# Attention and a gated feed-forward layer on one core: part of the weight conversion moved from VectorE to GpSimd, in pairs and in a new order

## The chip, the cores and the metric

The kernel runs on one core of one Trainium2 chip. The metric is the device time of one execution in microseconds, as the median of several runs. Engines are called by their names in the profile: PE (matrix multiply), DVE (VectorE), ACT (ScalarE), POOL (GpSimd), SP (the queue that issues all of this kernel's DMAs).

## The reference

```python
# q, k, v: (8, 8, 576, 64); p: (8, 8, 32, 64); w_in: (512, 2048); w_out: (2048, 512)
def sm_attn(qq, kk, vv):
    s = scale * np.matmul(qq, kk.transpose(0, 1, 3, 2))
    a = np.exp(s - np.max(s, axis=-1, keepdims=True))
    a = a / (np.sum(a, axis=-1, keepdims=True) + 1e-09)
    return np.matmul(a, vv)
p_packed = sm_attn(p, k, v)
out = sm_attn(q, p_packed, p_packed)

x = out.transpose(0, 2, 1, 3).reshape(4608, 512)
h = x @ w_in
g = h * np.tanh(softplus(h))          # Mish
return g @ w_out
```

The two weights arrive as float64; everything else is float32.

## The kernel before, in words

**Work.** There are 8 batches, and the hidden width of 2048 is cut into 16 groups of 128. The main loop makes one step `t` per batch and group: `up` multiplies the attention weights of the batch with a packed form of `w_in` (two halves `up(0)`, `up(1)`, six L627 matmuls each), ACT applies Mish (L630, L632) from PSUM, and `down` multiplies the result of an earlier group with `w_out` (four column blocks `down(0)` to `down(3)`; in batch 0 as one fp32 product, which is two L666 instructions). `LAG = 2` says that the downs of step t belong to the group of step t - 2. `packed_w(b, c)` multiplies the second attention's values into chunk c of `w_in` (four groups, 16 L577 matmuls), ACT and DVE split the product into a high and a low part (`wp_hi`, `wp_lo`). Chunks 1 to 3 of batch 0 are packed at t = 3, 7 and 11, ahead of the step that needs them. It needs two PSUM tiles of the pool `ps_a`, which also holds the scores of the next batch's attention; DVE frees those by reading them (L416, and L242 for the value product).

**Weights.** The float64 weights come as 32 pieces: `Weight(c, m)`, 16 of `w_in` (four for a chunk), and `WeightOut(i)`, 16 of `w_out` (one for a group). Each piece is 128 x 1024 words of 32 bits, with low and high words side by side. A piece goes through three steps. `fetch`: a DMA into a staging tile `w_st` (pool `stg`, `STB = 10` buffers). `words`: ACT reads the high words as floats scaled by 2^-112 into the destination (L547) and the low words, scaled by 2^-29, into a tile `wround` (L548). `join`: DVE clamps the scaled value (L552), shifts it by 3 bits (L555), ORs the sign bit from the high word in staging (L556), and adds the rounding (L559), all on 128 x 512.

**Order.** Batch 0's attention and the first four joined pieces stand before the loop (the opening). In the loop, `join_next` joins two pieces at each step t = 0 to 13, and `upto("fetch", k + 1 + STB)` fetches the piece that takes over the freed staging buffer. The pieces run wi, wi, wi, wi (chunk 0) and then wi and wo in turns, so that the last piece of chunk c is joined in the step whose `packed_w` reads it. The attention of batch 1 is a generator, moved on by `advance(gen)` three times a step from t = 2; `flush` runs the DVE work that was put off until the next point. The order on PE is the order of the program everywhere; on SP up to t = 16; on DVE and ACT from just before the loop up to t = 16. In the opening, a scheduler orders DVE and ACT.

**Loads.** Before step 0, SP also gets the first five loads for batch 1 (`load_next`: p, then k, k, q, q, v); later ones are issued as tiles come free. SP issues strictly in order, so a load stands behind every fetch written ahead of it, and a fetch behind the join that frees its buffer.

Of the kernel before, what the change touches and what calls it, by code (L numbers as in the profile page):

```python
# [10 lines left out]
I32 = mybir.dt.int32  # L11
U32 = mybir.dt.uint32
AF = mybir.ActivationFunctionType
ALU = mybir.AluOpType
# [3 lines left out]
GB = 3  # L18
KVB = 8
KQB = 5  # L20
STB = 10
OB = 2
ATT0 = 2
LOAD0 = 0
# [10 lines left out]
def body(  # L35
# [75 lines left out]
    def load_heads(src, b, g, tag):  # L111
        ts = []
        for h0 in (4 * g, 4 * g + 2):
            t = early.tile([R, 2, NI, 2 * D], F32, name=tag, tag="kvq", bufs=KVB)
            nc.sync.dma_start(
                out=t, in_=src[b, h0:h0 + 2].rearrange("h (p i x) d -> p h i (x d)", i=NI, x=2)
            )
            ts.append(t)
        return ts
# [411 lines left out]
    class Weight:  # L531
# [6 lines left out]
        def fetch(self):  # L538
            self.st = stg.tile([P, 2 * FC], I32, name="w_st")
            nc.sync.dma_start(out=self.st, in_=w_in_v[:, self.m, self.c * 2 * FC:(self.c + 1) * 2 * FC])  # L540
            self.dst = wi[self.c][self.m // 2][:, self.m % 2]

        def words(self):
            x = self.st.rearrange("p (n t) -> p n t", t=2)
            low, self.high = x[:, :, 0], x[:, :, 1]
            self.r = stg.tile([P, FC], I32, name="wround", bufs=3)
            nc.scalar.activation(out=self.dst, in_=self.high.bitcast(F32), func=AF.Copy, scale=F64_SCALE)  # L547
            nc.scalar.activation(out=self.r, in_=low.bitcast(U32), func=AF.Copy, scale=2.0 ** -29)  # L548

        def join(self):  # L550
            dst, bits = self.dst, self.dst.bitcast(I32)
            nc.vector.tensor_scalar(  # L552
                out=dst, in0=dst, scalar1=F64_HIGH, scalar2=-F64_HIGH, op0=ALU.min, op1=ALU.max
            )
            nc.vector.tensor_scalar(out=bits, in0=bits, scalar1=3, scalar2=None, op0=ALU.logical_shift_left)  # L555
            nc.vector.scalar_tensor_tensor(  # L556
                out=bits, in0=self.high, scalar=-0x80000000, in1=bits, op0=ALU.bitwise_and, op1=ALU.bitwise_or
            )
            nc.vector.tensor_tensor(out=bits, in0=bits, in1=self.r, op=ALU.add)  # L559

    class WeightOut(Weight):
        def __init__(self, i):
# [131 lines left out]
    def together(*gens):  # L694
        gens = list(gens)
        while gens:
            gens = [x for x in gens if next(x, "end") != "end"]
# [24 lines left out]
    n_groups = B * NF  # L722

    pieces = [Weight(0, m) for m in range(4)]
    for f in range(NF):
        if f < 12:
            pieces.append(Weight(1 + f // 4, f % 4))
        pieces.append(WeightOut(f))
    pieces_done = {"fetch": 0, "words": 0, "join": 0}

    def upto(step, n):
        while pieces_done[step] < min(n, len(pieces)):
            k = pieces_done[step]
            getattr(pieces[k], step)()
            pieces_done[step] += 1
            if step == "join":
                upto("fetch", k + 1 + STB)

    def join_next(n):
        for _ in range(n):  # L740
            k = pieces_done["join"]
            upto("words", k + 1)
            upto("join", k + 1)
            upto("words", k + 2)

    with tc.manual_schedule(engines={mybir.EngineType.PE}):
        for _ in range(8):
            nc.tensor.matmul(out=ps_warm, lhsT=still, rhs=still, start=True, stop=True)
        first = batches[0]
        by_hand = ExitStack()  # L750
        by_hand.enter_context(tc.manual_schedule(engines={mybir.EngineType.SP}))
        first.k_t = [load_heads(k, 0, 0, "k_t")]
        first.load_p()
        upto("fetch", 1)
        first.k_t.append(load_heads(k, 0, 1, "k_t"))
        first.v_t = [load_heads(v, 0, 0, "v_t")]
        first.q_t = [load_heads(q, 0, 0, "q_t")]
        upto("fetch", 2)
        first.v_t.append(load_heads(v, 0, 1, "v_t"))
        first.q_t.append(load_heads(q, 0, 1, "q_t"))  # L760
        upto("fetch", STB)
        first.start(ps_a)
        score = [first.score_now(g) for g in range(2)]
        for _ in range(3):
            next(score[0])
        upto("words", 1)
        next(score[0], None)
        upto("join", 1)
        next(score[1])
        next(score[1])  # L770
        together(first.turn_weights(0, ps_acc, ("ACT", "ACT")))
        next(score[1])
        next(score[1], None)
        together(first.values(0, ps_a))
        together(first.turn(0, ps_acc, ("ACT", "ACT", "ACT")))
        together(first.turn_values(0, ps_a))
        together(first.turn_weights(1, ps_acc, ("ACT", "ACT")))
        together(first.match(0, ps_acc))
        upto("words", 2)
        first.peak(slice(0, 1))  # L780
        first.rise(slice(0, 1))
        upto("join", 2)
        together(first.values(1, ps_a))
        together(first.turn(1, ps_acc, ("ACT", "ACT", "ACT")))
        together(first.turn_values(1, ps_a))
        together(first.match(1, ps_acc))
        upto("words", 3)
        first.peak(slice(1, 2))
        first.rise(slice(1, 2))
        first.weigh(slice(0, 1))  # L790
        upto("words", 4)
        upto("join", 4)
        wps = {(0, 0): packed_w(0, 0)}
        first.weigh(slice(1, 2))
        by_hand.enter_context(tc.manual_schedule(engines={mybir.EngineType.DVE, mybir.EngineType.Activation}))
        upto("words", 5)
        groups = []
        gen = iter(())
        g_rest = None
        for t in range(n_groups + LAG):  # L800
            b, f = divmod(t, NF)
            grp = None
            if t < n_groups:
                if f == 0:
                    if b % 2 == 0:
                        g_rest = ([], [])
                if f == (1 if b else ATT0) and b + 1 < B:
                    gen = batches[b + 1].attention()
                if t == LOAD0:
                    opening.close()  # L810
                    kv.append(ctx.enter_context(tc.tile_pool(name="kv", bufs=2, side="left", reuse_waits="tile")))
                    for _ in range(KQB):
                        load_next()
                grp = Group(b, f, wps[b, f // 4], g_rest)
                grp.tiles()
            groups.append(grp)
            dn = groups[t - LAG] if t >= LAG else None
            joins = 2 if t < 14 else 0
            if t == NF:
                by_hand.close()  # L820
            if t == SPLIT0:
                stage.close()
                late.append(ctx.enter_context(tc.tile_pool(name="late", bufs=1, side="right", reuse_waits="tile")))
            if 0 <= t - SPLIT0 < NF:
                split_wo(t - SPLIT0)
            if dn:
                down(dn, 0)
            if grp:
                grp.up(0)
            chunk = b == 0 and f % 4 == 3 and f < NF - 1  # L830
            if not chunk:
                advance(gen)
            join_next(joins - joins // 2)
            if dn:
                down(dn, 1)
                down(dn, 2)
            if chunk:
                flush()
                wps[0, f // 4 + 1] = packed_w(0, f // 4 + 1)
            else:  # L840
                advance(gen)
            if grp:
                grp.up(1)
                grp.halves()
            join_next(joins // 2)
            if dn and dn.b % 2 == 1 and dn.f % 4 == 2:
                rest["g"] = split(dn.g_rest[0][dn.f // 4], dn.g_rest[1][dn.f // 4])
            if dn:
                down(dn, 3)
            if grp and f % 4 == 2 and (b or f == NF - 2):  # L850
                nb, nch = divmod(b * (NF // 4) + f // 4 + 1, NF // 4)
                if nb < B:
                    flush()
                    if nb > b:
                        finish(gen)
                    wps[nb, nch] = packed_w(nb, nch)
            elif b == 0 and not chunk:
                advance(gen)
            if dn and dn.b % 2 == 1 and dn.f % 4 == 3:
                flush()  # L860
                down_rest(dn)
# [26 lines left out]
```

## Time and profile before

| | |
|---|---|
| median of 3 runs | 779.27 us (778.96 to 779.28) |
| the profiled execution | 777.98 us; span 776.2 us |
| busy in the span | PE 740.1 (95%), DVE 440.8 (57%), ACT 297.3 (38%), POOL 0.7 us (6 instructions) |
| chain that ended last | PE 85%, DVE 6%, DMA 5%, SP's queue 2% |
| DMA issues (KB each) | w_st 512 (x32), k_t, q_t, v_t 288 (12 in all, batch 0), p_t 64 (x2); a later batch: k_n and q_n 144 (8 each), v_n 128 (x8) and 64 (x2), p_n 32 (x4) |
| matmul clock granted | 0.988 over the span |

Busy PE time is not PE at its peak: the ends of matmuls are modelled, and in a crowded stretch they overlap. How long a run of matmuls takes is read from the chain of work, in order of time. "L577" is line 577 of the kernel; "a<-b" is output and input. In a list of waits the columns are: who waited, for whom, microseconds in total, times, longest. In a group row, the numbers behind the bar are busy time in us, mean ns of one, and idle time ahead of it.

### The profile page before, as it was taken

The numbers are of one execution on the slowest core, as the hardware profiler recorded it, in microseconds if no ns is written. First come the engines' busy times: TensorE is split into PE (matmuls) and PEld (weight loads), VectorE is DVE, ScalarE is ACT, GpSimd is POOL, SyncE is SP. The second block draws the span as 40 slices with busy tenths as digits, with TensorE's granted clock in tenths as the row PEclk, the third lists the DMA queues.
The fourth block names the chain that finished last, engine by engine and source line by source line (L and its number), as shares of the span: only waits on it lengthen the run. The fifth ranks groups of instructions, "written<-read, shape, count | busy, mean of one in ns | idle before, by whom it ended". The sixth has DMA issues, their size and how long they took to land.

```text
span 776.2 us, 12461 instructions
## 1 busy us (share of the span) xinstructions
PE 740.1 (95%) x5044; PEld 565.9 (73%) x5044; DVE 440.8 (57%) x788; ACT 297.3 (38%) x685; POOL 0.7 (0%) x6
## 2 busy tenths in 40 slices
PE   6777896999999999999999999999999999999997
PEld 4453553568788787878788787878788787888886
DVE  4888898964663636554663636554673636432332
ACT  3563654824242334224342244224242244322221
POOL 0000000000000000000000000000000000000000
PEclk9998998999999999999999999999999999999999
DMA  9999980032510534032510434032400200010002
GB/s 248 338 194 275 223 197 0 1 86 41 98 23 1 119 58 84 1 85 38 103 21 1 113 61 86 1 85 32 92 1 1 69 2 1 1 55 1 0 1 69
DMA packets 184825, 56.39 MB, mean 73 GB/s; under 512 B 173760, under 2 KB 176064, under 8 KB 184768
## 3 DMA queue, kind: packets, MB, share of 16 engines
q1 hardware_dynamic: 184768, 55.59, 30.8%
q8 instruction: 40, 0.66, 0.4%
q14 instruction: 17, 0.14, 0.1%
HBM read 46.14 MB, written 9.44 MB: 72 GB/s over the span
## 4 chain that ended last, share of the span: by engine, by line
PE 85%; DVE 6%; DMA 5%; SPq 2%; issue 1%; ACT 0%; DVEq 0%
PE ps_h L627 25%; PE acc L646 15%; PE acc L648 13%; PE acc L647 13%; PE ps_w L577 5%; PE acc L666 3%; DMA w_st<-in_moe_w_in_dram 3%; PE ps_s L396 2%; PE ps_rest L647 2%; PE ps_rest L648 2%; PE ps_rest L646 2%; SPq L341 2%; DMA w_st<-in_moe_w_out_dram 1%; PE ps_pp L451 1%; DVE xT L386 1%
## 5 line engine op out<-in xcount | busy, mean ns | idle before, releaser
L630 ACT ACTIVATE g<-ps_h 128x288 f32<-128x288 f32 (+1 forms) x256 | 97.6, 384 | 322.7 <-PE ps_h L627 293.3
L646 PE MATMUL acc<-wo_hi,g_hi 128*128 128x512 f32 x448 | 183.9, 410 | 0.0
L648 PE MATMUL acc<-wo_hi,g_lo 128*128 128x512 f32 x448 | 176.4, 394 | 0.0
L647 PE MATMUL acc<-wo_lo,g_hi 128*128 128x512 f32 x448 | 176.2, 393 | 0.0
L627 PE MATMUL ps_h<-aT_hi,wp_hi 128*128 128x288 f32 x512 | 165.2, 323 | 4.7 <-ACT aT_hi L297 4.7
L627 PE MATMUL ps_h<-aT_lo,wp_hi 128*128 128x288 f32 x512 | 152.8, 298 | 1.4 <-DVE aT_lo L300 1.4
L627 PE MATMUL ps_h<-aT_hi,wp_lo 128*128 128x288 f32 x512 | 152.0, 297 | 0.0
L641 DVE CAST g_hi<-g 128x512 fp32r<-128x512 f32 x112 | 47.6, 425 | 169.8 <-ACT g L630 169.6
L627 PEld LDWEIGHTS ps_h<-aT_hi,wp_hi 128*128 128x128 f32 x512 | 97.7, 191 | 27.1 <-issue 7.5
L646 PEld LDWEIGHTS acc<-wo_hi,g_hi 128*128 128x128 f32 x448 | 84.0, 187 | 43.4 <-issue 28.4
L627 PEld LDWEIGHTS ps_h<-aT_lo,wp_hi 128*128 128x128 f32 x512 | 97.8, 191 | 17.0 <-issue 6.0
L648 PEld LDWEIGHTS acc<-wo_hi,g_lo 128*128 128x128 f32 x448 | 84.0, 188 | 19.7
L627 PEld LDWEIGHTS ps_h<-aT_hi,wp_lo 128*128 128x128 f32 x512 | 97.7, 191 | 0.0
L647 PEld LDWEIGHTS acc<-wo_lo,g_hi 128*128 128x128 f32 x448 | 84.3, 188 | 9.0 <-issue 0.2
L642 DVE TENSOR_TENSOR g_lo<-g,g_hi 128x512 fp32r<-128x512 f32 x112 | 77.3, 690 | 6.3 <-DVE g_hi L641 0.5
L666 PE MATMUL acc<-wo,g 128*128 128x512 f32 x128 | 63.2, 609 | 0.0
L577 PE MATMUL ps_w<-wi,ppT 64*32 64x512 f32 x512 | 41.8, 634 | 15.1 <-DVE wi L559 7.1
L589 DVE TENSOR_TENSOR wp_lo<-ps_w,wp_hi 128x512 fp32r<-128x512 f32 x64 | 41.3, 683 | 24.8 <-ACT wp_hi L588 24.8
L588 ACT CAST wp_hi<-ps_w 128x512 fp32r<-128x512 f32 x64 | 34.4, 590 | 50.4 <-PE ps_w L577 50.4
L666 PEld LDWEIGHTS acc<-wo,g 128*128 128x128 f32 x128 | 22.7, 196 | 15.4 <-issue 13.8
L577 PEld LDWEIGHTS ps_w<-wi,ppT 64*32 64x32 f32 x512 | 7.6, 108 | 31.4 <-issue 17.1
L632 ACT ACTIVATE g_rest<-ps_h 128x64 f32<-128x64 f32 x128 | 28.1, 220 | 0.0
(107 smaller groups left out, 688.8 us busy)
## 6 DMA issues: line engine op xcount, KB each, us to landing
w_st<-in_moe_w_in_dram SPq DMA_DIRECT2D x16, 512.0 KB, 7.8
w_st<-in_moe_w_out_dram SPq DMA_DIRECT2D x16, 512.0 KB, 5.7
k_n<-in_k_dram SPq DMA_DIRECT2D x56, 144.0 KB, 3.1
q_n<-in_q_dram SPq DMA_DIRECT2D x56, 144.0 KB, 3.2
v_n<-in_v_dram SPq DMA_DIRECT2D x56, 128.0 KB, 2.8
out_dram<-o SPq DMA_DIRECT2D x28, 256.0 KB, 2.0
k_t<-in_k_dram SPq DMA_DIRECT2D x4, 288.0 KB, 5.0
v_t<-in_v_dram SPq DMA_DIRECT2D x4, 288.0 KB, 8.6
```

What stands on the lines that cost most here:

```text
L577: nc.tensor.matmul(out=ps[g][h * NP:(h + 1) * NP, :], lhsT=ppTb[row:row + D, g, h * NP:(h + 1) * NP], rhs=wi[c][g][row:row + D, h // 2, :] ...
L588: nc.scalar.copy(out=hi, in_=ps[g])
L589: nc.vector.tensor_tensor(out=lo, in0=ps[g], in1=hi.bitcast(F32), op=ALU.subtract)
L627: nc.tensor.matmul(out=ps, lhsT=w[:, fs], rhs=a[:, g, cs], start=(n == 0), stop=(n == 5))
L630: nc.scalar.activation(out=self.act[:, hf * HALF:hf * HALF + m], in_=ps[:, :m], func=AF.Mish)
L632: nc.scalar.activation(out=self.g_rest[self.b % 2][self.f // 4][:, self.f % 4, :], in_=ps[:, m:], func=AF.Mish)
L641: nc.vector.tensor_copy(out=hi, in_=self.act)
L642: nc.vector.tensor_tensor(out=lo, in0=self.act, in1=hi.bitcast(F32), op=ALU.subtract)
L646: nc.tensor.matmul(out=acc, lhsT=hi[:, cs], rhs=wh, start=start, stop=False)
L647: nc.tensor.matmul(out=acc, lhsT=hi[:, cs], rhs=wl, start=False, stop=False)
L648: nc.tensor.matmul(out=acc, lhsT=lo[:, cs], rhs=wh, start=False, stop=stop)
L666: nc.tensor.matmul(out=accs[c], lhsT=grp.act[:, cs], rhs=wo[f], start=f == 0, stop=f == NF - 1)
```

## The change

GpSimd takes over the clamp, and makes a sign word (0 or -2^31) in place of the high word in staging. The rounding goes back into the low word in staging, so `wround` is gone and a staging tile stays in use until the add. On DVE one instruction shifts and ORs, a second adds; the pieces are joined in pairs, whose instructions alternate. The staging has 11 buffers.

The pieces have a new order: the wi pieces of a chunk stand two by two among the wo pieces, and the last one of a chunk has index 9, 17 and 25 instead of 10, 18 and 26. Six pieces are joined ahead of the loop instead of four, and step t joins up to 2t + 8 and prepares the words up to 2t + 12, for t = 0 to 12. So the last wi piece of a chunk is joined at t = 1, 5 and 9. The downs of batch 0 follow one step behind the up instead of two; at t = 17 no down is made, and after that the lag is 2 as before. At a `packed_w` of batch 0, the third down stands behind it instead of ahead of it. The first fetch goes out ahead of everything, POOL's order is by hand in the loop as well.

```diff
-STB = 10
+STB = 11
...
-            self.r = stg.tile([P, FC], I32, name="wround", bufs=3)
             nc.scalar.activation(out=self.dst, in_=self.high.bitcast(F32), func=AF.Copy, scale=F64_SCALE)
-            nc.scalar.activation(out=self.r, in_=low.bitcast(U32), func=AF.Copy, scale=2.0 ** -29)
+            nc.scalar.activation(out=self.low, in_=self.low.bitcast(U32), func=AF.Copy, scale=2.0 ** -29)
+            nc.gpsimd.tensor_scalar(
+                out=self.dst, in0=self.dst, scalar1=F64_HIGH, scalar2=-F64_HIGH, op0=ALU.min, op1=ALU.max
+            )
+            nc.gpsimd.tensor_scalar(
+                out=self.high, in0=self.high, scalar1=0.0, scalar2=-2.0 ** 31, op0=ALU.is_lt, op1=ALU.mult
+            )
 
         def join(self):
             dst, bits = self.dst, self.dst.bitcast(I32)
-            nc.vector.tensor_scalar(
-                out=dst, in0=dst, scalar1=F64_HIGH, scalar2=-F64_HIGH, op0=ALU.min, op1=ALU.max
-            )
-            nc.vector.tensor_scalar(out=bits, in0=bits, scalar1=3, scalar2=None, op0=ALU.logical_shift_left)
             nc.vector.scalar_tensor_tensor(
-                out=bits, in0=self.high, scalar=-0x80000000, in1=bits, op0=ALU.bitwise_and, op1=ALU.bitwise_or
-            )
-            nc.vector.tensor_tensor(out=bits, in0=bits, in1=self.r, op=ALU.add)
+                out=bits, in0=bits, scalar=3, in1=self.high, op0=ALU.logical_shift_left, op1=ALU.bitwise_or
+            )
+            yield
+            nc.vector.tensor_tensor(out=bits, in0=bits, in1=self.low, op=ALU.add)
...
-    for f in range(NF):
-        if f < 12:
-            pieces.append(Weight(1 + f // 4, f % 4))
-        pieces.append(WeightOut(f))
...
+    pieces += [WeightOut(0), Weight(1, 0), Weight(1, 1), WeightOut(1), Weight(1, 2), Weight(1, 3)]
+    pieces += [WeightOut(2), WeightOut(3)]
+    for c in (2, 3):
+        for e in range(2):
+            pieces += [Weight(c, 2 * e), Weight(c, 2 * e + 1), WeightOut(4 * c - 4 + 2 * e), WeightOut(4 * c - 3 + 2 * e)]
+    pieces += [WeightOut(i) for i in range(12, NF)]
...
+    def join(n):
+        words(n)
+        together(*[x.join() for x in pieces[done["join"]:n]])
+        done["join"] = max(done["join"], min(n, len(pieces)))
+        fetch(n + STB)
...
-            dn = groups[t - LAG] if t >= LAG else None
-            joins = 2 if t < 14 else 0
+            lag = 1 if t <= NF else LAG
+            dn = groups[t - lag] if t >= lag and t != NF + 1 else None
...
-            join_next(joins - joins // 2)
+            if t <= 12:
+                join(2 * t + 8)
+                words(2 * t + 12)
             if dn:
                 down(dn, 1)
-                down(dn, 2)
             if chunk:
                 flush()
                 wps[0, f // 4 + 1] = packed_w(0, f // 4 + 1)
-            else:
+            if dn:
+                down(dn, 2)
+            if not chunk:
                 advance(gen)
...
-            join_next(joins // 2)
```

How this moves instructions shows at three places. The first is DVE just ahead of the spread of the first scores of batch 1 (L412 to L416), at t = 3; `packed_w` of chunk 1 (`wi_0_93`, `wi_1_94`) follows on PE. Before:

```order
L386 STREAM_TRANSPOSE xT<-k_n 128x1152
L552 TENSOR_SCALAR wo_163<-wo_163 128x512
L555 TENSOR_SCALAR wo_163<-wo_163 128x512
L556 SCALAR_TENSOR_TENSOR wo_163<-w_st,wo_163 128x512
L559 ISA wo_163<-wo_163,wround 128x1024
L552 TENSOR_SCALAR wi_1_94<-wi_1_94 128x512
L555 TENSOR_SCALAR wi_1_94<-wi_1_94 128x512
L556 SCALAR_TENSOR_TENSOR wi_1_94<-w_st,wi_1_94 128x512
L559 ISA wi_1_94<-wi_1_94,wround 128x1024
L412 TENSOR_REDUCE mx<-ps_s_672 128x1
L412 TENSOR_REDUCE mx<-ps_s_673 128x1
L414 TENSOR_TENSOR top<-mx 128x1
```

After, at the same place:

```order
L386 STREAM_TRANSPOSE xT<-k_n 128x1152
L557 SCALAR_TENSOR_TENSOR wi_0_95<-wi_0_95,w_st 128x512 x2
L561 ISA wi_0_95<-w_st,wi_0_95 128x1024 x2
L412 TENSOR_REDUCE mx<-ps_s_698 128x1
L412 TENSOR_REDUCE mx<-ps_s_699 128x1
L414 TENSOR_TENSOR top<-mx 128x1
```

Eight piece instructions are now four, and they belong to chunk 2 (`wi_0_95`); chunk 1 was finished ahead of the two L386.

The second place is DVE at the end of the opening, between the first peak (L273) and the last low part of batch 0's attention (L300), for which the first full up on PE waits. Before, its last rows are:

```order
L287 RECIPROCAL sm_476<-sm_476 128x18
L288 TENSOR_TENSOR a_348<-a_348,sm_476 128x576
L294 STREAM_TRANSPOSE at<-a_348 128x576
L300 TENSOR_TENSOR aT_lo<-at,aT_hi 128x576
L552 TENSOR_SCALAR wo_153<-wo_153 128x512
```

After:

```order
L287 RECIPROCAL sm_474<-sm_474 128x18
L288 TENSOR_TENSOR a_358<-a_358,sm_474 128x576
L557 SCALAR_TENSOR_TENSOR wo_158<-wo_158,w_st 128x512
L561 ISA wi_0_93<-w_st,wi_0_93 128x1024
L294 STREAM_TRANSPOSE at<-a_358 128x576
L561 ISA wo_158<-w_st,wo_158 128x1024
L300 TENSOR_TENSOR aT_lo<-at,aT_hi 128x576
L557 SCALAR_TENSOR_TENSOR wi_1_94<-wi_1_94,w_st 128x512 x2
```

Pieces 6 and 7 now stand inside this end of the opening, and pieces 4 and 5 a little further ahead, where before only the rest of piece 4 stood.

The third place is SP at the start.

```order
-L884 UNCONDITIONAL_BRANCH
+L889 UNCONDITIONAL_BRANCH
+L540 DMA w_st<-in_moe_w_in_dram 128x1024
 L115 DMA k_t<-in_k_dram 96x2x384 x2
 L170 DMA p_t<-in_p_dram 128x2x64 x2
+L115 DMA k_t<-in_k_dram 96x2x384 x2
 L540 DMA w_st<-in_moe_w_in_dram 128x1024
-L115 DMA k_t<-in_k_dram 96x2x384 x2
 L115 DMA v_t<-in_v_dram 96x2x384 x2
```

The first weight piece is issued ahead of k_t; and further on, 17 pieces instead of 14 are fetched ahead of the loads for batch 1.

More of the change, by code (lines that the diff above doesn't have):

```diff
@@ L544, in words @@
             x = self.st.rearrange("p (n t) -> p n t", t=2)
-            low, self.high = x[:, :, 0], x[:, :, 1]
-            self.r = stg.tile([P, FC], I32, name="wround", bufs=3)
+            self.low, self.high = x[:, :, 0], x[:, :, 1]
             nc.scalar.activation(out=self.dst, in_=self.high.bitcast(F32), func=AF.Copy, scale=F64_SCALE)
-            nc.scalar.activation(out=self.r, in_=low.bitcast(U32), func=AF.Copy, scale=2.0 ** -29)
+            nc.scalar.activation(out=self.low, in_=self.low.bitcast(U32), func=AF.Copy, scale=2.0 ** -29)
[5 more added lines that the diff above has]
+            )
         def join(self):
             dst, bits = self.dst, self.dst.bitcast(I32)
-            nc.vector.tensor_scalar(
-                out=dst, in0=dst, scalar1=F64_HIGH, scalar2=-F64_HIGH, op0=ALU.min, op1=ALU.max
-            )
-            nc.vector.tensor_scalar(out=bits, in0=bits, scalar1=3, scalar2=None, op0=ALU.logical_shift_left)
-            nc.vector.scalar_tensor_tensor(
-                out=bits, in0=self.high, scalar=-0x80000000, in1=bits, op0=ALU.bitwise_and, op1=ALU.bitwise_or
-            )
-            nc.vector.tensor_tensor(out=bits, in0=bits, in1=self.r, op=ALU.add)
+            nc.vector.scalar_tensor_tensor(
+                out=bits, in0=bits, scalar=3, in1=self.high, op0=ALU.logical_shift_left, op1=ALU.bitwise_or
+            )
+            yield
+            nc.vector.tensor_tensor(out=bits, in0=bits, in1=self.low, op=ALU.add)
     class WeightOut(Weight):
@@ L724, in body, with fetch, words @@
     pieces = [Weight(0, m) for m in range(4)]
-    for f in range(NF):
-        if f < 12:
-            pieces.append(Weight(1 + f // 4, f % 4))
-        pieces.append(WeightOut(f))
[L729 to L744, printed above, removed]
+    pieces += [WeightOut(0), Weight(1, 0), Weight(1, 1), WeightOut(1), Weight(1, 2), Weight(1, 3)]
[4 more added lines that the diff above has]
+    pieces += [WeightOut(i) for i in range(12, NF)]
+    done = {"fetch": 0, "words": 0, "join": 0}
+    def fetch(n):
+        for x in pieces[done["fetch"]:n]:
+            x.fetch()
+        done["fetch"] = max(done["fetch"], min(n, len(pieces)))
+    def words(n):
+        for x in pieces[done["words"]:n]:
+            x.words()
+        done["words"] = max(done["words"], min(n, len(pieces)))
+    def join(n):
[3 more added lines that the diff above has]
+        fetch(n + STB)
     with tc.manual_schedule(engines={mybir.EngineType.PE}):
@@ L751, in body @@
         by_hand.enter_context(tc.manual_schedule(engines={mybir.EngineType.SP}))
+        fetch(1)
         first.k_t = [load_heads(k, 0, 0, "k_t")]
         first.load_p()
-        upto("fetch", 1)
         first.k_t.append(load_heads(k, 0, 1, "k_t"))
+        fetch(2)
         first.v_t = [load_heads(v, 0, 0, "v_t")]
         first.q_t = [load_heads(q, 0, 0, "q_t")]
-        upto("fetch", 2)
+        fetch(3)
         first.v_t.append(load_heads(v, 0, 1, "v_t"))
         first.q_t.append(load_heads(q, 0, 1, "q_t"))
-        upto("fetch", STB)
+        fetch(STB)
         first.start(ps_a)
@@ L765, in body @@
             next(score[0])
-        upto("words", 1)
         next(score[0], None)
-        upto("join", 1)
         next(score[1])
         next(score[1])
+        join(2)
         together(first.turn_weights(0, ps_acc, ("ACT", "ACT")))
@@ L778, in body @@
         together(first.match(0, ps_acc))
-        upto("words", 2)
         first.peak(slice(0, 1))
         first.rise(slice(0, 1))
-        upto("join", 2)
         together(first.values(1, ps_a))
@@ L786, in body @@
         together(first.match(1, ps_acc))
-        upto("words", 3)
+        join(4)
         first.peak(slice(1, 2))
@@ L790, in body @@
         first.weigh(slice(0, 1))
-        upto("words", 4)
-        upto("join", 4)
         wps = {(0, 0): packed_w(0, 0)}
         first.weigh(slice(1, 2))
-        by_hand.enter_context(tc.manual_schedule(engines={mybir.EngineType.DVE, mybir.EngineType.Activation}))
-        upto("words", 5)
+        words(8)
+        join(6)
+        by_hand.enter_context(tc.manual_schedule(engines={mybir.EngineType.DVE, mybir.EngineType.Activation, mybir.EngineType.Pool}))
+        words(10)
         groups = []
```

## The prediction

> **What bounds the kernel now.** I read the page first: which engines are busy, and in which slices.
>
> ```profile
> PE   6777896999999999999999999999999999999997
> ...
> DVE  4888898964663636554663636554673636432332
> ...
> POOL 0000000000000000000000000000000000000000
> ```
>
> From slice 7 (136 us) on PE is at 9 and DVE below it: there only less matrix work would help. In slices 0 to 5 PE is at 6 to 8 and DVE at 8 or 9, while POOL does nothing. The change works in those slices, so I asked next what PE waited for between 44 and 130 us, and when.
>
> ```profile
> PE ps_w L577 <- DVE wi L559: 7.1, 1, 7.1
> PE ps_w L577 <- DVE a L416: 5.6, 1, 5.6
> PE ps_w L577 <- DVE pp L242: 2.4, 1, 2.4
> ```
>
> ```profile
> 43.94 0.45 PE L627 MATMUL ps_h<-aT_hi,wp_lo 128*128 128x288 f32 x1
> ...
> 119.58 1.07 PE L577 MATMUL ps_w<-wi,ppT 64*32 64x512 f32 x10
> 127.75 1.92 PE L577 MATMUL ps_w<-wi,ppT 64*32 64x512 f32 x6 [7.11 <-DVE wi L559]
> 129.61 0.61 PE L627 MATMUL ps_h<-aT_hi,wp_hi 128*128 128x288 f32 x1
> ```
>
> All three are `packed_w` of the next chunk (steps t = 3, 7, 11), and all three end on DVE: on the last wi piece, or on the attention step that queued behind pieces and frees the PSUM tile. What the stretch from 43.94 to 129.61 (85.7 us) should cost comes from the chain where PE runs freely, and its counts from the groups of that window.
>
> ```profile
> 129.68 1.74 PE ps_h L627 x6
> 131.41 2.22 PE acc L666 x4
> ...
> 139.45 1.72 PE acc L666 x4
> 141.17 0.80 PE ps_h L627 x6
> ...
> 147.85 1.02 PE ps_w L577 x16
> ...
> 165.62 0.65 PE ps_s L396 x16
> ...
> 182.31 0.44 PE ps_a L438 x4
> ...
> 197.08 0.83 PE ps_pp L451 x40
> ```
>
> ```profile
> L666 PE MATMUL acc<-wo,g 128*128 128x512 f32 x78 | 38.8, 611 | 0.0
> L627 PE MATMUL ps_h<-aT_hi,wp_hi 128*128 128x288 f32 x45 | 20.6, 458 | 0.0
> L548 ACT ACTIVATE wround<-w_st 128x512 int32<-128x512 uint32 x23 | 15.7, 681 | 0.0
> ```
>
> A down is two L666, 0.86 us; 78 make 39 downs, 33.5 us. An up is six L627, 0.80; 45 of one of the three kinds make 22.5 ups, 18.0. Three `packed_w` 3.1, four score pairs 2.6, two value products 1.7, twelve transposes of 0.11 1.3. Sum 60.2: the stretch loses 25.5 us, 15.1 in the three waits, the rest in short waits and restarts (after the third wait an up takes 1.74 and two downs 2.22 instead of 0.80 and 1.72, 1.4 lost).
>
> DVE in it, by windows, and what one piece takes of it:
>
> ```profile
> core 0: us, PE busy (x) PEld busy (x) DVE busy (x) ACT busy (x) POOL busy (x), PEclk, DMA share, GB/s
> 0.00:28.00 28.00, 19.36 (x163) 13.84 (x163) 14.05 (x40) 13.64 (x30) 0.70 (x6) 1.00 0.97 289
> 28.00:44.00 16.00, 9.45 (x107) 5.62 (x100) 13.63 (x27) 6.49 (x11) 0.00 (x0) 1.00 0.97 261
> 44.00:64.00 20.00, 13.49 (x68) 8.80 (x67) 17.27 (x32) 10.55 (x24) 0.00 (x0) 0.92 1.02 234
> 64.00:94.00 30.00, 27.46 (x171) 15.12 (x178) 25.32 (x47) 18.45 (x36) 0.00 (x0) 0.94 0.92 231
> 94.00:128.00 34.00, 26.89 (x181) 14.81 (x170) 29.70 (x50) 17.23 (x33) 0.00 (x0) 0.91 0.59 139
> ```
>
> ```profile
> L559 DVE CUSTOM_DVE_ANT_0 wi<-wi,wround 128x1024 uint16<-128x1024 uint16 x11 | 7.6, 693 | 1.5
> L556 DVE SCALAR_TENSOR_TENSOR wi<-w_st,wi 128x512 int32<-128x512 int32 x11 | 7.6, 692 | 0.4
> ...
> L556 DVE SCALAR_TENSOR_TENSOR wo<-w_st,wo 128x512 int32<-128x512 int32 x11 | 7.6, 688 | 0.3
> ...
> L555 DVE TENSOR_SCALAR wi<-wi 128x512 int32<-128x512 int32 x11 | 4.7, 423 | 0.3
> ...
> L552 DVE TENSOR_SCALAR wi<-wi 128x512 f32<-128x512 f32 x11 | 4.5, 408 | 0.0
> ...
> L288 DVE TENSOR_TENSOR a<-a,sm 128x1152 f32<-128x1152 f32 x1 | 1.4, 1358 | 0.0
> L273 DVE TENSOR_TENSOR a<-a,mx 128x1152 f32<-128x1152 f32 x1 | 1.4, 1357 | 0.0
> ```
>
> DVE is busy 17.27 + 25.32 + 29.70 = 72.3 of 84 us; 22 pieces (11 wi, 11 wo) at 0.69 + 0.69 + 0.42 + 0.41 = 2.21 are 48.6 of it.
>
> **The change part by part.** *Clamp and shift leave DVE.* Each piece saves 0.83, 22 pieces 18.3: DVE has 72.3 - 18.3 = 54.0 left, less than PE's work. The fused shift-or is costed like L556 (the same form, 0.69), the add like L559. The add now reads the low word in staging with a gap: between 0.69 (L556 also reads staging with a gap, and takes no longer) and 1.2 (if a gap halved the rate of the 16-bit form). I take 0.69; at 1.2 DVE would have 65, just PE's work.
>
> *New order, pairs, lag 1.* A chunk's last wi piece is joined two steps before its `packed_w` instead of in the same step, so the 7.1 us wait goes. The waits on L416 and L242 shrink with DVE's backlog; what is late next is DVE's spread at t = 3, behind six pieces. For the three places together, between 0 (the `packed_w` at 147.85 follows on without a gap) and 15.1, I keep 3.5, nearer to the first, since DVE has slack. With lag 1 four more downs (3.4 us) lie before the point at 129.61: 63.6 us of work instead of 60.2, and as much less after it.
>
> *GpSimd's two instructions per piece, and a new wait.* The fused step waits on POOL; behind it on DVE stand kT copies, maxima and spreads, for which PE waits. Inside the loop the two steps between words and join cover it. The nearest rows:
>
> ```profile
> 0.73 0.20 POOL masks.py:197 MEMSET ident<- 128x128 f32 x1 [0.29 <-POOLq L873]
> 1.00 0.29 POOL masks.py:199 TENSOR_SCALAR_AFFINE_SELECT ident<-ident 128x128 f32<-128x128 f32 x1
> ```
>
> Stretched to 512 columns the select gives 4 x 0.29 = 1.17 if all of it grows; with 0.10 as fixed (an estimate, half of the MEMSET) 0.10 + 4 x 0.19 = 0.87; the MEMSET likewise 0.50. I take 0.87, from the row that reads and writes: 1.74 per piece, 38.3 for 22, for which POOL has room in 65 us.
>
> No row shows POOL beside DVE. If a POOL instruction and a DVE one with two SBUF inputs run freely together, this costs 0. If they must take turns, the stretch needs 22 x (1.38 + 1.74) + 2.7 (L273 and L288) = 71.3, which is 6.3 over PE's 65.0 (63.6 and 1.4 of cold start). I take half, 3.
>
> The Trainium skill (SBUF — State Buffer, "Who interferes with whom") says that the second of the two to issue blocks until the first is done; by it the term is the full 6.3, and no run here shows it yet. The Trainium skill's GPSIMD Engine Reference, section 3.1, gives 769 ns for a tight loop over 512 elements; with that price the turns would need 66.9, 1.9 over PE.
>
> *Opening.* The first weight goes out ahead of k_t, and DVE has more pieces before the last aT_lo.
>
> ```profile
> 29.05 0.65 DVE L556 SCALAR_TENSOR_TENSOR wi<-w_st,wi 128x512 int32<-128x512 int32 x1
> ...
> 30.54 0.68 DVE L559 CUSTOM_DVE_ANT_0 wi<-wi,wround 128x1024 uint16<-128x1024 uint16 x1
> ...
> 42.72 0.76 DVE L300 TENSOR_TENSOR aT_lo<-at,aT_hi 128x576 fp32r<-128x576 f32 x1 [0.74 <-ACT aT_hi L297]
> ```
>
> Between 28 and 43.5 these two are all the piece work; the new order has pieces 4 to 7 there, 4 x 1.38 = 5.5, so 4.2 more on an engine that was busy 13.63 of 16. Some 1.2 falls into its gaps; 512 KB ahead of k_t are 1.8 us at 289 GB/s, of which I count 1.5. The loop starts 4.5 us later, between 1.5 (DVE's part hidden in its waits on ACT) and 7 (POOL collides as well). ACT makes five more pieces there, at two L548-like instructions of 0.68 each 6.8 us, free since it is busy 6.49 of the 16. The deeper staging (11) costs nothing by itself: weights only go earlier into a queue that is full anyway.
>
> *Sum.* 43.94 + 4.5 + 65.0 + 3.5 + 3 = 119.9 for the point at 129.61: 9.7 earlier, with 3.4 less work behind it and without the cold restart there, 1.4: 14.5 off. The profiled execution is 777.98 (span 776.2 and 1.8 around it), 1.3 under the median of the runs, 779.27. 779.3 - 14.5 = **765**.
>
> **Rivals.**
> *Slower: taking turns with a dear POOL.* Full turns need 22 x (1.38 + 2P) + 2.7. Without the 3 counted above the gain is 17.5, so it is gone at a stretch of 65.0 + 17.5 = 82.5, that is P = 1.12 us per instruction. At P = 1.17, the straight stretch of the select, 84.5: 781; at 1.3, 787. For it: two operations per element, one of them on integers. Against: the select has a comparison in it too, at 0.29. 14 in 100.
>
> *Full turns at 0.87*: 6.3 instead of 3, 768; 13 in 100. The Trainium skill's rule above is this case.
>
> *No collision*: POOL works while DVE reduces, transposes and waits; the 3 and up to 3 of the opening's 4.5 return: 759 to 762, and 756 with the 3.5 gone too. 17 in 100.
>
> *Weights arrive too late.* ACT now reads four pieces ahead of the joins, in order, before the next Mish.
>
> ```profile
> w_st<-in_moe_w_in_dram SPq DMA_DIRECT2D x16, 512.0 KB, 7.8
> ```
>
> Piece 17 goes out behind 17 pieces of 0.52 MB, batch 0's 3.7 and batch 1's first loads of 3.1: with itself 16.2 MB. By the windows above 8.1 + 4.2 = 12.3 MB are in at 44, and 234 GB/s bring the rest by 61; ACT reaches it at t = 3, about 64. The DMA share is 0.9 to 1.0 up to 94 us, so it cannot hurry. Should the stream fall behind by one landing time, 7.8, at one step, 772. 6 in 100.
>
> *No change* (gains and losses meet): 4 in 100.
>
> **How the numbers follow.** The forecast, 763 to 767, has 46 in 100. What a measurement can tell from no change is 0.2%, 1.6 us. Slower is the first rival, 14; same 4; the rest, 82, is faster. The range goes from the third rival with all covers, a little under 756, to the foot of the slower one: 753 to 780. Outside it are about 2 in 10, nearly all above.
>
> **What would show it.** POOL: 64 L548/L551 rows near 0.87 us; over 1.1 the slower rival gains. DVE: L557 and L561 at 0.69; rows of 1 us and more mean blocking. PE: the wait of 7.1 us before the third `packed_w` gone, the first two under 2; the loop's first full-speed up near 48; DVE under 60 us in the 70 behind it. ACT's words waiting on w_st near 60 us would be the DMA rival. From the second batch on nothing should differ. I am wrong if POOL's rows are long, if the opening slips by 8 us or more, or if another DVE step takes the place of the wi pieces.

## The result, and the profile after

The changed kernel takes 768.8 us, the median of four runs (765.87 to 769.94), against 779.27 us before: ratio 0.9857, 95% interval 0.9827 to 0.9887. The forecast was 765. The profiled execution took 769.94 us (span 768.1), the longest of the four; the span of before was 776.2, so the two profiles differ by 8.1 us.

Busy tenths by slice, of the page after:

```profile
PE   6559998999999999999999999999999999999997
...
DVE  3496869673744647373753737463663637433332
...
POOL 3769894000000000000000000000000000000000
```

Against before, slices 1 and 2 of PE fell from 7, 7 to 5, 5, and slices 3 to 6 rose from 7, 8, 9, 6 to 9, 9, 9, 8: the opening grew longer and the loop behind it shorter. POOL is at 6 to 9 in slices 1 to 5.

PE's rows in order of time that answer to the two ends of the stretch (the same points as before: 43.94 and 129.61):

```profile
52.88 0.44 PE L629 MATMUL ps_h<-aT_hi,wp_lo 128*128 128x288 f32 x1
...
123.37 1.09 PE L579 MATMUL ps_w<-wi,ppT 64*32 64x512 f32 x16
124.39 1.12 PE L668 MATMUL acc<-wo,g 128*128 128x512 f32 x2
124.95 0.69 PE L629 MATMUL ps_h<-aT_hi,wp_hi 128*128 128x288 f32 x1
```

The third `packed_w` follows without a gap; its 7.1 us wait is gone. The stretch is 72.1 us instead of 85.7. It starts 8.9 us later, ends 4.7 sooner, and what follows takes 643.15 (768.1 - 124.95) instead of 646.6: 4.7 + 3.4 = 8.1.

What PE still waits for between 30 and 132 us:

```profile
PE ps_h L629 <- ACT wp_hi L590: 4.8, 1, 4.8
PE ps_a L221 <- ACT qT L133: 3.6, 1, 3.6
PE ps_h L629 <- ACT aT_hi L297: 3.6, 1, 3.6
PE ps_w L579 <- DVE a L416: 1.9, 1, 1.9
...
PE acc L668 <- DVE wo L561: 1.6, 1, 1.6
```

The first three lie in the opening. Of the three waits of 15.1 us one of 1.9 is left, and wo brings a new one of 1.6. Counted by the rows of the add, the opening now joins 8 pieces (5 before) and the stretch 20 (22 before): part of the stretch's work has moved into the longer opening.

The groups of POOL, and two of DVE's (busy us, mean ns, idle ahead and its cause):

```profile
L551 POOL TENSOR_SCALAR w_st<-w_st 128x512 int32<-128x512 int32 x32 | 69.1, 2161 | 2.5
L548 POOL TENSOR_SCALAR wo<-wo 128x512 f32<-128x512 f32 x16 | 12.5, 780 | 7.7 <-ACT wo L546 6.6
L548 POOL TENSOR_SCALAR wi<-wi 128x512 f32<-128x512 f32 x16 | 12.4, 773 | 18.7 <-ACT wi L546 17.8
```

```profile
L561 DVE CUSTOM_DVE_ANT_0 wi<-w_st,wi 128x1024 uint16<-128x1024 uint16 x16 | 12.9, 830 | 0.2
L557 DVE SCALAR_TENSOR_TENSOR wi<-wi,w_st 128x512 int32<-128x512 int32 x16 | 11.9, 759 | 4.9 <-POOL w_st L551 4.8
```

The sign word takes 2.16 us, the clamp 0.78: 2.94 per piece where the forecast had 1.74. On DVE the two steps of a piece take 0.76 and about 0.84 instead of 0.69 each, and wait for POOL. The rows of one place show both, first of DVE, then of POOL:

```profile
53.54 1.28 DVE L561 CUSTOM_DVE_ANT_0 wi<-w_st,wi 128x1024 uint16<-128x1024 uint16 x2
...
60.69 0.69 DVE L557 SCALAR_TENSOR_TENSOR wo<-wo,w_st 128x512 int32<-128x512 int32 x1 [2.58 <-POOL w_st L551]
61.30 2.14 DVE L561 CUSTOM_DVE_ANT_0 wo<-w_st,wo 128x1024 uint16<-128x1024 uint16 x2
```

```profile
60.74 1.12 POOL L548 TENSOR_SCALAR wi<-wi 128x512 f32<-128x512 f32 x1
61.94 2.33 POOL L551 TENSOR_SCALAR w_st<-w_st 128x512 int32<-128x512 int32 x1
...
71.02 0.61 POOL L548 TENSOR_SCALAR wo<-wo 128x512 f32<-128x512 f32 x1
71.72 1.98 POOL L551 TENSOR_SCALAR w_st<-w_st 128x512 int32<-128x512 int32 x1
```

A pair of adds takes 1.28 where POOL is idle for most of it; beside L551 it takes 2.14. POOL's own rows beside these steps of DVE are longer too: 2.33 against 1.98, 1.12 against 0.61.

In the opening ACT stood for weights that had not landed, with qT copies behind them in its order:

```profile
25.15 0.67 ACT L546 ACTIVATE wi<-w_st 128x512 f32<-128x512 f32 x1 [2.99 <-DMA w_st<-in_moe_w_in_dram]
...
27.98 0.66 ACT L546 ACTIVATE wo<-w_st 128x512 f32<-128x512 f32 x1 [1.61 <-DMA w_st<-in_moe_w_out_dram]
...
37.14 1.27 ACT L133 COPY qT<-ps_kq 128x384 f32<-128x384 f32 x3
```

Between the last two, ACT makes the words of five more pieces. Before, the last three qT copies start between 30.54 and 31.82; PE's wait of 3.6 us above is for these copies.

### The profile page after: what moved, and what is told of

Same layout as the page of the kernel before. It is cut to its first block, busy times and chain, and to the rows that moved or that the text cites. A ratio compares the mean times of both kernels' runs of the same rounds, so it can differ in the third digit from the quotient of the medians.

```text
span 768.1 us, 12501 instructions
## 1 busy us (share of the span) xinstructions
PE 734.5 (96%) x5044; PEld 563.3 (73%) x5044; DVE 421.5 (55%) x724; ACT 297.4 (39%) x685; POOL 94.7 (12%) x70
## 4 chain that ended last, share of the span: by engine, by line
PE 87%; DMA 3%; ACT 3%; DVE 3%; issue 1%; POOL 1%; SPq 0%; ACTq 0%; DVEq 0%; POOLq 0%
PE ps_h L629 25%; PE acc L648 15%; PE acc L650 14%; PE acc L649 14%; PE acc L668 5%; PE ps_w L579 4%; PE ps_s L396 3%; PE ps_rest L650 2%; PE ps_rest L649 2%; PE ps_rest L648 2%; DMA w_st<-in_moe_w_out_dram 2%; PE ps_pp L451 1%; DMA q_t<-in_q_dram 1%; ACT w_st L547 1%; DMA k_t<-in_k_dram 1%
## 5 line engine op out<-in xcount | busy, mean ns | idle before, releaser
L551 POOL TENSOR_SCALAR w_st<-w_st 128x512 int32<-128x512 int32 x32 | 69.1, 2161 | 2.5
L591 DVE TENSOR_TENSOR wp_lo<-ps_w,wp_hi 128x512 fp32r<-128x512 f32 x64 | 41.4, 683 | 23.4 <-ACT wp_hi L590 23.4
L579 PE MATMUL ps_w<-wi,ppT 64*32 64x512 f32 x512 | 38.0, 615 | 1.9 <-DVE a L416 1.9
```

What stands on the lines that cost most here:

```text
L551: nc.gpsimd.tensor_scalar(out=self.high, in0=self.high, scalar1=0.0, scalar2=-2.0 ** 31, op0=ALU.is_lt, op1=ALU.mult)
L579: nc.tensor.matmul(out=ps[g][h * NP:(h + 1) * NP, :], lhsT=ppTb[row:row + D, g, h * NP:(h + 1) * NP], rhs=wi[c][g][row:row + D, h // 2, :] ...
L591: nc.vector.tensor_tensor(out=lo, in0=ps[g], in1=hi.bitcast(F32), op=ALU.subtract)
```

## The experiments

Each is an edit to the kernel before or to the changed one; the ratio is to the kernel before, timed on the same chip at the same time, with its 95% interval. Times of different experiments come from up to four chips, on which the kernel before takes 778.0 to 779.2 us, so small differences between them are better read from the ratios. The first four name these theories: A, the forecast's (order and unloading both bring something, and the shortfall is in the opening's loads); B, the opening is set by waits for POOL; C, the order alone brings it; D, the unloading alone; E, L551 is long because it reads integers; F, because of its gap of a word or because it writes integers.

**Which half brought it: the order without GpSimd (`e2_nopool`).**

```
 words(): - nc.gpsimd.tensor_scalar(... min, max)
          - nc.gpsimd.tensor_scalar(... is_lt, mult)
 join():  + nc.vector.tensor_scalar(... min, max); yield
          + nc.vector.tensor_scalar(... logical_shift_left 3); yield
          ~ nc.vector.scalar_tensor_tensor(... bitwise_and -0x80000000, bitwise_or); yield
```

> The changed kernel's order, pairs and lag, but the clamp, shift and sign on DVE as before (four DVE instructions per piece, nothing on POOL). Theory A (order and unloading both needed): DVE carries 18 us more between the opening and the third packed product, so that it is as long as PE's work there and some waits come back: 3 to 8 us slower than the changed kernel, 772 to 777. Rival C (the order alone did it): 766 to 769, and the opening shorter since nothing waits on POOL. Rival D (unloading alone did it): 779 or more.

769.38 us, ratio 0.989 (0.9875 to 0.9906). With everything back on DVE the new order is as fast as the changed kernel within the intervals. Its windows from 44 us, with the columns of the prediction's table (each time its window, then PE, PEld, DVE, ACT, POOL), and its rows at the two ends of the stretch:

```profile
44.00:64.00 20.00, 14.04 (x47) 9.15 (x48) 16.14 (x30) 10.56 (x21) 0.00 (x0) 0.69 1.04 224
64.00:94.00 30.00, 29.46 (x196) 16.46 (x195) 24.27 (x50) 20.21 (x42) 0.00 (x0) 1.00 0.98 234
94.00:128.00 34.00, 30.01 (x200) 15.95 (x200) 28.80 (x54) 18.94 (x38) 0.00 (x0) 1.00 0.51 115
```

```profile
52.43 0.44 PE L629 MATMUL ps_h<-aT_hi,wp_lo 128*128 128x288 f32 x1
...
123.39 0.69 PE L629 MATMUL ps_h<-aT_hi,wp_hi 128*128 128x288 f32 x1
```

The opening ends at 52.43 and the stretch is 71.0 (the changed kernel: 52.88 and 72.1). So the short stretch does not need POOL: of the theories, C comes nearest, though the time is above its range and the opening is not shorter. The opening is as long without POOL, but that does not clear POOL in the changed kernel: here DVE has its work and is busy 15.95 of the 16 us from 28 to 44, and 10 pieces are joined before the opening ends (18 in the stretch); in the changed kernel DVE is busy 12.58 there.

**The unloading without the order (`e3_oldorder`).** The kernel before, with the changed kernel's `words` and its fused step; pieces, joins and lags stay old.

```
 words(): + the two nc.gpsimd.tensor_scalar of the changed kernel
 join():  - clamp, shift, and/or    + one shift-or
```

> The kernel before with the two POOL instructions and the fused step, but in the old order of pieces, one by one, words one piece ahead, lag 2. Theory A: a piece takes POOL 2.9 us (0.78 and 2.16), two pieces a step 5.9, and the last wi piece of a chunk is still joined in the step that needs it, so the three waits stay and DVE waits on POOL: 775 to 785. Rival D (unloading alone did it): 768 to 770.

787.95 us, ratio 1.013 (1.0113 to 1.0147): slower than before. DVE's waits between 40 and 135 us:

```profile
DVE wo L557 <- POOL w_st L551: 12.3, 7, 4.7
DVE wi L557 <- POOL w_st L551: 11.0, 6, 2.6
```

The old order prepares one piece ahead, and POOL's 2.94 us stand between words and join: 23.3 us of waiting in 13 places, against 5.5 in the changed kernel, which prepares four ahead. D falls, and the time is above A's range too.

**The opening's loads as before (`e1_loads`).**

```
-        fetch(1)
         first.k_t = [load_heads(k, 0, 0, "k_t")]
         first.load_p()
+        fetch(1)
         ... (second and third weight likewise one place later)
```

> The changed kernel with the loads of the opening in the order that they had before (k_t, p_t, then the first weight; third weight behind q_t). Theory A (the shortfall lies in the opening, and its first 2.5 us come from the first weight standing ahead of k_t and p_t): the first transpose of p starts near 6.0 us instead of 8.5, the first full-speed up 1 to 2.5 us earlier than 53.1, total 766 to 768. Theory B (the opening is set by the waits on POOL, not by loads): the start of p moves, the first full-speed up stays within 0.5 us of 53.1, total as the changed kernel, 768.8.

768.77 us, ratio 0.9883 (0.9865 to 0.9901); the opening ends at 50.61. The order of the loads is worth nothing that these runs can tell: the next kernel, which keeps the new loads, has 50.51 where the changed kernel has 52.88, so an opening moves by 2 us without any change to the loads. A falls as far as the loads go; B, that POOL sets the opening, is not decided.

**Sign from a float view (`e4_floatsign`).** `in0=self.high.bitcast(F32)` in L551.

> The changed kernel, but the sign word on POOL is made from the high word read as a float instead of an integer (still written as an integer). Theory E (reading integers makes that instruction 2 us long): it falls from 2.16 to between 0.6 and 1.2 us, POOL per piece to under 2; the waits on POOL in the opening (2.9 us) and at t = 2 and 3 (0.99, 2.58, 1.88) mostly go, and the total falls by 1 to 5 us, 764 to 768. Theory F (the gap between words, or writing integers, makes it long): it stays near 2 us and the total at 768.8.

```profile
L551 POOL TENSOR_SCALAR w_st<-w_st 128x512 int32<-128x512 f32 x32 | 69.4, 2167 | 2.5
```

767.75 us, ratio 0.9868 (0.9853 to 0.9883), and the row is no shorter. E falls. Whether the gap, the integer output or the pair of operations makes it long was not tried.

**GpSimd only clamps (`e5_clamponly`).** L551 is left out; DVE shifts, then ANDs and ORs as in the kernel before.

> Edit to the changed kernel: GpSimd only clamps; VectorE makes the sign and shifts as in the kernel before (shift 0.42, and/or 0.69, add 0.69 us for a piece). With nothing at all on GpSimd the new order gave 769.4. If unloading VectorE matters where VectorE is late (its opening: six pieces, 0.42 us each), 766 to 767.5. If unloading is worth nothing, 768.5 to 770. If any GpSimd instruction beside VectorE costs more than it saves (collisions at 1.1 us), 770 or more.

768.79 us, ratio 0.9879 (0.986 to 0.9898). With 23.4 us on POOL instead of 94 the time is the same. With the new order it makes no difference that can be measured whether DVE does four steps of a piece, three or two.

**What in the order does it.** The remaining runs take the order apart. First, from the kernel before, only more joins ahead (`e6_lead`):

```
-        upto("words", 5)
+        upto("words", 6); upto("join", 6); upto("words", 7)
```

> Edit to the kernel before: two pieces more are joined before the loop (six instead of four); nothing else, so VectorE still has every step, the pieces stand in the old order, one by one. Theory 'lead' (the weights that a packed product needs are finished turns ahead instead of in the same turn): the three waits before packed_w, 15.1 us, go for the most part, less up to 4.4 us (two pieces of 2.2) in the opening: 768 to 773. Rival 'the rest of the new order is needed' (pairs, piece order, the down product one turn sooner): 777 to 781, up to 783 if the 4.4 us aren't hidden.

778.78 us, ratio 1.0008 (0.9999 to 1.0018): nothing. PE's waits:

```profile
PE ps_w L577 <- DVE a L416: 5.6, 1, 5.6
PE ps_h L627 <- DVE wp_lo L589: 4.5, 1, 4.5
PE ps_w L577 <- DVE pp L242: 1.8, 1, 1.8
```

The last wi piece is on time and the third `packed_w` follows without a gap (121.77), but the wait of 7.1 has become one of 4.5 for the low part of the same product, behind the same queue on DVE. Of 15.1 us of waits 11.9 remain, and the opening ends 2.2 us later (46.17). Being ahead by two pieces does not help an engine that then has as much to do in every step.

Then the new order without GpSimd (769.4), one part undone at a time: the joins one after the other (`e11_nopair`),

```
-        together(*[x.join() for x in pieces[done["join"]:n]])
+        for x in pieces[done["join"]:n]:
+            together(x.join())
```

> Edit to the new order with nothing on GpSimd (769.4): the joins of two pieces stand one after the other instead of step beside step. Theory 'pairs': VectorE spends about 0.36 us more on each of 22 pieces between the opening and the last packed product of the first batch, 8 us, part of it in its idle time: 772 to 777. Rival 'pairs are worth nothing, the place of the steps in the turn is what counts': 768.5 to 770.5.

777.79 us, ratio 0.9984 (0.9975 to 0.9994), a little above the first theory's range: nearly all of the gain is gone. DVE's rows for two wo pieces, first in pairs (`e2_nopool`), then one by one (`e11_nopair`):

```profile
72.41 0.75 DVE L551 TENSOR_SCALAR wo<-wo 128x512 f32<-128x512 f32 x2
73.08 0.76 DVE L555 TENSOR_SCALAR wo<-wo 128x512 int32<-128x512 int32 x2
73.75 1.29 DVE L557 SCALAR_TENSOR_TENSOR wo<-w_st,wo 128x512 int32<-128x512 int32 x2
74.95 1.29 DVE L561 CUSTOM_DVE_ANT_0 wo<-w_st,wo 128x1024 uint16<-128x1024 uint16 x2
```

```profile
72.01 0.42 DVE L551 TENSOR_SCALAR wo<-wo 128x512 f32<-128x512 f32 x1
72.46 0.43 DVE L555 TENSOR_SCALAR wo<-wo 128x512 int32<-128x512 int32 x1
72.92 0.69 DVE L557 SCALAR_TENSOR_TENSOR wo<-w_st,wo 128x512 int32<-128x512 int32 x1
73.65 0.69 DVE L561 CUSTOM_DVE_ANT_0 wo<-w_st,wo 128x1024 uint16<-128x1024 uint16 x1
74.26 0.42 DVE L551 TENSOR_SCALAR wo<-wo 128x512 f32<-128x512 f32 x1
...
75.90 0.69 DVE L561 CUSTOM_DVE_ANT_0 wo<-w_st,wo 128x1024 uint16<-128x1024 uint16 x1
```

Busy times hardly differ; the distances do. A step that needs the one ahead of it starts 0.45 us after it; two that don't need each other stand 0.34 apart (0.67 for two). So two pieces take 3.83 us from the first start to the last end (72.41 to 76.24) instead of 4.58 (72.01 to 76.59): 0.38 for each of 22 pieces is 8.3 us. The runs differ by 8.4, or by 7.3 if one goes by the ratios (they are from two chips). PE does not lose this piece by piece. Up to the second `packed_w` the two kernels keep step; there DVE's backlog reaches PE, first in `e2_nopool`, then in `e11_nopair`:

```profile
93.90 1.79 PE L579 MATMUL ps_w<-wi,ppT 64*32 64x512 f32 x16
```

```profile
96.94 1.95 PE L579 MATMUL ps_w<-wi,ppT 64*32 64x512 f32 x14 [2.41 <-DVE pp L242]
```

The stretch ends at 128.75 instead of 123.39; the rest of the loss lies behind it.

The old list of pieces (`e7_oldpieces`): `pieces` alternates wi and wo as in the kernel before, all else as in `e2_nopool`.

> Edit to the new order with nothing on GpSimd (769.4): the list of pieces is the old one (wi and wo by turns), everything else new. The last piece of a chunk is then asked for one turn ahead of its packed product instead of two. Theory 'lead': one turn is enough, 768.5 to 771. Rival 'piece order': the waits before packed_w come back in part (2 to 7 us each for two or three of them), 774 to 779.

771.78 us, ratio 0.9918 (0.9903 to 0.9933): 2.4 us of the 9, a little over what the first theory allowed. The waits before `packed_w` do not come back; one of 3.7 us for the low part of the product does (1.3 in `e2_nopool`).

The down product two turns behind again (`e9_lag2`):

```
-            lag = 1 if t <= NF else LAG
-            dn = groups[t - lag] if t >= lag and t != NF + 1 else None
+            dn = groups[t - LAG] if t >= LAG else None
```

> Edit to the new order with nothing on GpSimd (769.4): the down product stands two turns behind its up product again, as in the kernel before. Theory 'pairs' (two pieces side by side spare VectorE the gap between steps that need each other, 2.36 us a piece before against about 2.0): lag is worth nothing here, 768.5 to 770.5. Rival 'the sooner down product fills TensorE while VectorE works': the waits before packed_w come back, 773 to 778. It may also gain, since each wo is then due a turn later (the wait of 2.7 us for wo near 119 us goes): 766.5 to 768.

771.7 us, ratio 0.9914 (0.99 to 0.9927): 2.3 us, between the two theories. Before `packed_w` PE waits 0.3 us.

The pairs alone, in the kernel before (`e12_pairs`). The edit also moves the second join of a step from its end to its first half, where the new order has both:

```
 join():  + a yield behind each of the first three steps
 upto():  + together() for two joins
-            join_next(joins - joins // 2)      ... -            join_next(joins // 2)
+            join_next(joins)
```

> Edit to the kernel before: the two joins of a turn stand together and step beside step (clamp of both, shift of both, and so on), early in the turn; pieces three and four of the opening likewise. Old piece order, old down product, four pieces in the opening, nothing on GpSimd, staging as before. Theory 'pairs carry the gain': a piece costs VectorE 1.87 us instead of 2.25 to 2.36 (in the loop's rows of the two kernels), 8.4 to 10.8 us over 22 pieces, and the opening stays at 44 us: 768 to 771. Rival 'pairs pay only with the other parts of the new order (two pieces more ahead, the packed product between two parts of the down product)': 774 to 778.

782.04 us, ratio 1.0048 (1.003 to 1.0066): slower, and both theories missed. One row of DVE's waits between 40 and 135 us, and three of PE's between 30 and 150:

```profile
DVE wo L552 <- ACT wo L547: 9.4, 5, 3.8
```

```profile
PE ps_w L580 <- DVE wi L562: 6.7, 1, 6.7
PE ps_w L580 <- DVE a L416: 6.0, 1, 6.0
...
PE ps_w L580 <- DVE pp L242: 2.2, 1, 2.2
```

The same wait was 1.9 us, once, in the kernel before. With words prepared one ahead of the joins, the second piece of a pair is not ready: ACT makes its words in order behind a Mish, and that waits for PE. 7.5 us more of waiting for ACT is about what the pairs spare, and the three waits before `packed_w` are all there. So pairs alone bring nothing here, and `e11_nopair`, which has the rest of the new order without them, gains little. That words made ahead are what the pairs lack is read from these waits, not shown: the last wi piece of a chunk is also still joined in the step that needs it, and part of ACT's lateness follows from PE's own waits. Pairs with words ahead and nothing else were not run.

**The opening.** `e8_shortopen` takes two pieces out of the opening of `e2_nopool`:

```
-        words(8)
-        join(6)
+        words(6)
 ...
-        words(10)
+        words(8)
 ...
-            if t <= 12: join(2 * t + 8); words(2 * t + 12)
+            if t <= 13: join(2 * t + 6); words(2 * t + 10)
```

> Edit to the new order with nothing on GpSimd (769.4): the opening joins four pieces instead of six and prepares eight instead of ten; the loop's requests stand two pieces later throughout. Theory 'the opening's 9 us come from the work put ahead of the second weigh step on VectorE and ScalarE': the opening ends 3 to 5 us sooner (two pieces of 2.2 us on VectorE) and the loop's stretch stays near 70.7: 764.5 to 767. Rival 'the loop needs that lead': the stretch grows by as much, 768 to 772.

788.68 us, ratio 1.013 (1.0111 to 1.0149), and not to be read as a time of this order: with the down product one turn behind, the first column block of steps 3, 5, 7, 9 and 11 takes a wo piece ahead of its join, so five products use weights that are not finished, and DVE then waits for PE to have read them:

```profile
DVE wo L551 <- PE acc L668: 13.3, 2, 7.2
```

Its opening still counts: it ends at 48.46 instead of 52.43. `e10_shortlag2` makes the same edit with the down product two turns behind, where every piece is joined in time.

> As the edit above (down product two turns behind, nothing on GpSimd), and the opening joins four pieces instead of six and prepares eight instead of ten. Theory 'the opening's 9 us are the work put ahead of the second weigh step': full speed near 48 instead of 52.7 us; with each wo due a turn later that lead is not missed: 764 to 767. Rival 'the loop needs the lead': 768.5 to 773.

767.4 us (765.77 to 769.71), ratio 0.986 (0.9839 to 0.988), just above the first theory's range. The row that ends the opening:

```profile
48.72 0.44 PE L629 MATMUL ps_h<-aT_hi,wp_lo 128*128 128x288 f32 x1
```

Against `e9_lag2` the time falls by 4.3 us and the opening by 3.5 (52.22 to 48.72): two pieces less of joins on DVE and of words on ACT, ahead of the second `weigh` step, are about that. The version also narrows what in the order counts: in program order it has the lag of the kernel before and joins no further ahead (four pieces before the loop, up to 2t + 6 in step t), so neither is needed for the gain. What it has over `e12_pairs` is words four ahead, the last wi piece of a chunk joined a step before its `packed_w`, the third down behind `packed_w`, the staging and the order of the first loads; these were not taken apart. It is the best version without GpSimd. Its interval overlaps that of the changed kernel, which no version here beats by more than can be told.

## Why the prediction was right, and where not

The time was right to 4 us, within the range. The reason given for most of it was not. In the profiled executions 8.1 of the 14.5 us came: the opening is 4.4 us worse than its term, the stretch 0.6 and what follows 1.4. Two of the prediction's own signs of being wrong showed, POOL's long rows and an opening later by 8 us or more, and the time still fell in the range; that is in part luck. (In its first reading, DVE is at 4 in slice 0 and at 9 in slice 7, and PE at 9 in slice 5; nothing rests on it.)

*Clamp and shift leave DVE (18.3 us).* The arithmetic nearly held: in the stretch DVE is busy 55.2 us, where 54.0 were forecast, with 20 pieces of some 1.57 us and not 22 of 1.38. The step that failed is what it was taken for. DVE has the room (16.20 + 23.59 + 27.08 = 66.9 us of the 84 from 44 to 128, some 6 of them weigh steps of the opening that slipped past 44), and the order without any unloading, with DVE busy for 69.2, is as fast within the intervals, which leave 2 or 3 us at most to the unloading. Unloading in the old order makes the kernel 9.5 us slower (787.95 against 778.5).

*New order, pairs, lag 1.* The prediction costed pairs at nothing: it added up DVE's durations, 2.21 a piece, which is what a piece takes alone, and not the distances of the starts in a pair. By the run that undoes them, pairs are worth 7 to 8 us in the order without GpSimd, nearly the whole gain, and by `e12_pairs` nothing without the rest. In the changed kernel itself, where only two steps of a piece are left on DVE, the pairs were not undone; whether the unloading would stand in for them there is open. The residual waits of 3.5 came out at 1.9 + 1.6, but the 1.6 is a wait for wo before a down, which the term did not name. The 7.1 wait goes when the last wi piece is joined sooner, as forecast, but by `e6_lead` that alone gives nothing, since other waits on DVE take its place.

*POOL's price.* 0.87 per instruction was taken from a select of 128 columns; it is 1.47 in the mean (0.78 and 2.16), outside the bounds of 0.50 and 1.17. The slower rival was to decide from 1.12, and it did not. Its condition was met and its mechanism was too strong.

*Taking turns (3).* Full turns at the measured price need 22 x (1.38 + 2.94) + 2.7 = 97.7 us; the stretch took 72.1. The Trainium skill's rule (SBUF — State Buffer, "Who interferes with whom"), an exclusive lock on the ports that the two share, read as in the prediction (the second of the two blocks until the first is done), is not what the rows show: the adds at 61.30 end at 63.44 while L551 runs from 61.94 to 64.27. They slow each other (1.07 for 0.64, 2.33 for 1.98), which on the 24 pieces between 44 and 128 us, 37.6 us in four groups or 1.57 each, is about 24 x (1.57 - 1.38) = 4.6 us of DVE time, and DVE had room for it. The 3 in the sum stood close to the stretch (71.5 forecast, 72.1 measured) but only because the two errors, in price and in blocking, met: luck.

*Opening (+4.5, between 1.5 and 7).* This term was mis-sized: 8.9 in the profiled execution, 6.6 in `e4_floatsign` with the same order. The order of the first loads is not the cause as far as the runs can tell. What they show, without GpSimd, is DVE's and ACT's piece work ahead of the second weigh step: 3.5 to 4 us for two pieces, in two pairs of runs. In the changed kernel, where DVE is not full, the rows point to the ACT part, five words costed at nothing since ACT was busy 6.49 of 16 us: it has waits for loads in it (2.99 and 1.61 us), and the last qT copies stand behind it until 37.14. No run undoes that, so how much is POOL's and how much ACT's stays open. Even with two pieces fewer the opening of `e10_shortlag2` is 4.8 us longer than before; its rows show 8 pieces joined where before there were 5, and pT and the first xT of batch 1 (0.44 and 1.37 us) ahead of the last aT_lo.

*Behind the point (3.4 + 1.4).* 3.4 measured, as much as the four downs moved ahead; the 1.4 of the cold restart does not show in the time.

*Late weights.* ACT has no wait for w_st near 60 us; that rival showed in the opening only.

## What to carry to other kernels

Cost an engine that is nearly full by the distances between its starts, not by its durations: steps that need each other start further apart than steps that don't, and interleaving two independent pieces gets the difference back (here 0.38 us of 2.3 a piece). Such an interleaving can look worthless alone, and so can the order that lets it work (here without pairs 1 us, pairs alone a loss of 4), so test them together as well as apart. Moving work to an idle engine is worth what the full engine does with the time; before doing it, put the same new order on the old engine.

## What the runs showed of the hardware

- GpSimd's min-max on 128x512 f32 takes 0.61 us with no two-input VectorE step on 128x512 beside it, less than the 0.87 estimated; the is_lt-mult in place with a step of two words takes 1.98, and the same 2.17 in the mean with float as with integer input.
- GpSimd and VectorE slow each other down by parts: a two-input VectorE step of 0.64 (in a pair) takes 1.07 beside L551, L551 2.33 instead of 1.98, the clamp 1.12 instead of 0.61.
- On VectorE a step that depends on the one ahead of it starts 0.45 us behind it where an independent one of 0.42 starts 0.34 behind. The Trainium skill (VectorE: DVE Perf Modes, "The DRAIN you can't avoid") states that eight copies take as long with a semaphore after each as with one after the last; the rows of this case, with other operations, each of which needs the one ahead, show 0.11 a step.
